# Block-sparse attention and MoE on one core: computing 352 of 768 key columns per query tile, with the division behind the product with the values

## The chip, the cores and the metric

The kernel runs on one core of a Trainium2 chip. A core has five engines with a queue each: TensorE (PE, with PEld for its weight loads), VectorE (DVE), ScalarE (ACT), GpSimd (POOL) and SyncE (SP, which here only issues DMAs). The metric is the device time of one execution in microseconds; smaller is better. The kernel before took 878.65 us in the median of three runs (877.41 to 878.98).

## The reference

Four batches, eight heads, 768 positions, head dimension 64. Attention is masked by blocks of 32 positions: a query block sees its neighbours, the first and the last block, and three sampled blocks; the first and the last query block see everything. The result goes through a two-layer network with a parametric ReLU. Q, K and V are float32, the weights float64, the sampled blocks int64.

```python
scores = scale * np.matmul(q, k.transpose(0, 1, 3, 2))
mask = np.abs(blk_i - blk_j) <= window
mask = mask | (blk_i == 0) | (blk_j == 0) | (blk_i == n_blocks - 1) | (blk_j == n_blocks - 1)
for qb in range(n_blocks):
    for kb in sampled_blocks[qb]:
        mask[qb * block:(qb + 1) * block, kb * block:(kb + 1) * block] = True
scores = np.where(mask, scores, -1000000000.0)
attn = np.exp(scores - np.max(scores, axis=-1, keepdims=True))
attn = attn / (np.sum(attn, axis=-1, keepdims=True) + 1e-09)
x = np.matmul(attn, v)      # then (3072, 512): tokens x heads * 64
h = x @ w_in                # 512 x 2048
out = (np.maximum(h, 0.0) + alpha * np.minimum(h, 0.0)) @ w_out
```

## The kernel before

**Numbers.** float32 is carried as a pair of float16 parts, upper and lower, after a scaling by a power of two. A product is the sum of three (MoE, values) or four (scores) float16 products in the same PSUM. For the scores, upper and lower parts of a head lie side by side on the 128 partitions, and `ks` is K with its two halves swapped: Q against `kt` and against `ks` gives all four terms.

**Attention.** A unit is two heads, with two tiles of 128 queries; a step is one head and one tile, 192 in all. A step multiplies Q with all 768 keys (`emit_s`, L558: four matmuls of 512 and 256 columns), adds the mask and finds the extreme in one VectorE instruction (`emit_bias`, L568), takes the exponential on ScalarE (L575), makes the reciprocal of the sum (L579, L583), makes upper and lower parts of the normalised probabilities (`emit_p_hi`, L348/L350/L352; `emit_p_lo`, L356 on VectorE or L358 and L359 on GpSimd; a table `PL` sends two of three to GpSimd) and transposes both by DMA on SP's queue (L598). `emit_av` (L633) then multiplies with V for a whole unit: 36 matmuls with 64-wide weights, the two heads in the two halves of the array. The output lies transposed already, as the MoE needs it (`x`, L644 and L649).

**MoE.** A chunk is two query tiles with all eight heads (12 chunks). Eight times it does an up block (`emit_up`, L947: 24 matmuls of 256 columns into `h`, of which there is one buffer), `emit_act` on VectorE (L957, L958), the upper part `gh` on ScalarE (L963), the lower part `gl` on GpSimd (L968), and a down block (`emit_down`, L986: 12 matmuls of 512 columns).

**The start.** The weights come as float64, 512 KB a piece, and are made into float32 by integer steps (`emit_n1`, `emit_n2`, `emit_n3`: L805, L812 or L810, L817) on VectorE, then into float16 parts (`emit_w_hi`, `emit_w_lo`; for `w_in` the lower part goes over TensorE, L873 and L874). K and Q of the first units are transposed by TensorE (L480, L483, L498).

**Order.** Nothing of the order is written out by hand. Every piece of work is a `plan.op` with a priority, a cost per engine, its dependences and its buffers; `Plan.run` plays these through with its own costs and so fixes each engine's order. On the chip each engine then takes its instructions strictly in that order. The buffer counts stand in `BUFS` (L42) and in the PSUM pools (L211 to L215).

## Time and profile before

| | |
|---|---|
| runs | 878.65 us in the median of three, 877.41 to 878.98 |
| profiled execution | span 876.4 us from its first to its last instruction; the profile gives no other time of its own |
| mean granted TensorE clock | 0.961 |
| DMA packets | 381844, 133.80 MB |

The profile is one execution on the chip. Its page gives each engine's busy time, the span in 40 slices, the DMA queues, and groups of instructions by line. "Windows" give busy times in chosen stretches, the "timeline" instructions in order, "waits" who waited for whom. In rows of the timeline the first two numbers are start and duration in us; a matmul's duration contains its way through the array, so its price in a stream is the distance from start to start.

### The profile page before, as it was taken

What the parts mean: (1) busy time and instruction counts of PE and PEld (TensorE: products, weight loads), DVE (VectorE), ACT (ScalarE), POOL (GpSimd) and SP (SyncE); (2) the same over time, 40 slices, a digit from 0 to 9 for tenths busy, and PEclk for the clock granted to TensorE, in tenths of its full rate; (3) what the DMA queues carried; (4) which work ended last, traced back from release to release, by engine and by line L of the source; (5) the groups of instructions that cost most, each with busy time, mean ns of one, the idle gap of its engine ahead of it and who ended that gap; (6) DMA issues with size and microseconds to landing.
All of it is one profiled execution on the core that took longest, in us unless ns stands there. A gap on an engine that the chain in (4) does not pass through costs nothing.

```text
span 876.4 us, 17097 instructions
## 1 busy us (share of the span) xinstructions
PE 802.7 (92%) x6249; PEld 533.7 (61%) x6249; DVE 672.0 (77%) x1395; ACT 554.9 (63%) x1188; POOL 560.4 (64%) x458
## 2 busy tenths in 40 slices
PE   3856476999999999999999999999999999999997
PEld 2423134666766666676666666667666666766664
DVE  3889989999977778779877777788787787666322
ACT  4886677877656777566746866666667774565111
POOL 3294676777846786767757867667467867666121
PEclk9878567999999999999999999999999999999999
DMA  7877778799799797877889979888997986776200
GB/s 234 243 189 188 195 156 149 125 171 169 167 174 172 145 176 142 182 144 145 187 154 177 148 149 155 179 143 163 189 183 142 175 132 114 122 132 109 37 25 25
DMA packets 381844, 133.80 MB, mean 153 GB/s; under 512 B 346404, under 2 KB 375104, under 8 KB 381760
## 3 DMA queue, kind: packets, MB, share of 16 engines
q1 hardware_dynamic: 345728, 90.74, 61.1%
q10 hardware_dynamic: 35968, 41.95, 16.7%
q8 instruction: 49, 0.80, 0.4%
q14 instruction: 35, 0.29, 0.1%
q0 software_dynamic: 64, 0.02, 0.0%
HBM read 35.67 MB, written 6.29 MB: 48 GB/s over the span
## 4 chain that ended last, share of the span: by engine, by line
PE 63%; DVE 14%; issue 8%; POOL 6%; ACT 6%; ACTq 2%; DMA 1%; POOLq 0%; DVEq 0%
PE h L947 21%; PE o L986 21%; PE sp L558 10%; PE av L633 8%; DVE e L568 2%; ACT e L575 2%; POOL ph L359 2%; ACTq L387 2%; POOL gl L968 2%; DVE wo L817 1%; DVE g L957 1%; POOL e L358 1%; ACT ph L348 1%; DVE g L958 1%; DVE qn L426 1%
## 5 line engine op out<-in xcount | busy, mean ns | idle before, releaser
L947 PE MATMUL h<-x,wi 128*128 128x256 f16 x2304 | 267.2, 273 | 7.3 <-DVE g L958 7.3
L947 PEld LDWEIGHTS <-wi 128*128 128x128 f16 x2304 | 225.0, 98 | 47.9 <-issue 10.2
L986 PE MATMUL o<-wo,gh 128*128 128x512 f16 x768 | 228.5, 379 | 0.0
L575 ACT ACTIVATE e<-e,nm 128x768 f32<-128x768 f32 x192 | 178.6, 930 | 74.6 <-DVE nm L568 65.7
L359 POOL TENSOR_TENSOR ph<-e,ph 128x768 f16<-128x768 f32 x128 | 217.9, 1702 | 10.7
L568 DVE CUSTOM_DVE_ANT_0 e<-sp,bias,cs 128x768 f32<-128x768 f32 x192 | 192.0, 1007 | 26.2 <-PE sp L558 16.6
L358 POOL TENSOR_SCALAR e<-e,rs 128x768 f32<-128x768 f32 x128 | 132.0, 1032 | 110.4 <-ACT ph L348 60.4
L968 POOL TENSOR_TENSOR gl<-g,gh 128x512 f16<-128x512 f32 x96 | 117.9, 1228 | 115.0 <-ACT gh L963 107.4
L963 ACT CAST gh<-g 128x512 f16<-128x512 f32 x96 | 59.2, 616 | 140.6 <-DVE g L958 130.6
L986 PE MATMUL o<-wo,gl 128*128 128x512 f16 x384 | 145.5, 379 | 0.6 <-POOL gl L968 0.6
L957 DVE TENSOR_SCALAR g<-h,am 128x256 f32<-128x256 f32 x192 | 83.6, 476 | 78.5 <-PE h L947 78.1
L558 PEld LDWEIGHTS <-qt 128*128 128x128 f16 x768 | 74.2, 102 | 84.9 <-issue 32.1
L986 PEld LDWEIGHTS <-gh 128*128 128x128 f16 x768 | 74.7, 98 | 78.6 <-issue 0.8
L558 PE MATMUL sp<-kt,qt 128*128 128x512 f16 (+1 forms) x384 | 98.9, 341 | 21.6 <-DVE nm L568 19.4
L348 ACT ACTIVATE ph<-e,rs 128x768 f16<-128x768 f32 x110 | 101.6, 926 | 12.3 <-DVE rs L583 5.8
L633 PE MATMUL av<-pt,v 128*64 128x256 f16 x1728 | 105.9, 278 | 0.0
L633 PEld LDWEIGHTS <-v 128*64 128x64 f16 x1728 | 92.1, 111 | 18.9 <-issue 16.1
L558 PE MATMUL sp<-ks,qt 128*128 128x512 f16 (+1 forms) x384 | 98.4, 339 | 0.0
L356 DVE SCALAR_TENSOR_TENSOR ph<-e,rs,ph 128x768 f16<-128x768 f32 x64 | 76.6, 1197 | 11.1 <-ACT ph L348 10.6
L958 DVE SCALAR_TENSOR_TENSOR g<-h,gsc,g 128x512 f32<-128x512 f32 x96 | 72.1, 751 | 3.4
L986 PEld LDWEIGHTS <-gl 128*128 128x128 f16 x384 | 37.6, 98 | 46.3 <-POOL gl L968 1.1
L352 POOL TENSOR_SCALAR ph<-e,rs 128x768 f16<-128x768 f32 x38 | 45.1, 1186 | 30.5 <-DVE rs L583 21.7
(132 smaller groups left out, 755.0 us busy)
## 6 DMA issues: line engine op xcount, KB each, us to landing
wo<-in_moe_w_in_dram ACTq DMA_DIRECT2D x16, 512.0 KB, 5.0
raw<-in_moe_w_out_dram ACTq DMA_DIRECT2D x16, 512.0 KB, 4.0
kf<-in_k_dram ACTq DMA_DIRECT2D x16, 384.0 KB, 4.2
qf<-in_q_dram ACTq DMA_DIRECT2D x48, 128.0 KB, 4.3
vf<-in_v_dram ACTq DMA_DIRECT2D x16, 384.0 KB, 5.2
out_dram<-ob ACTq DMA_DIRECT2D x24, 256.0 KB, 4.2
ks<-kt SPq DMA_DIRECT2D x24, 192.0 KB, 3.9
pt<-ph SPq DMA_TRANSPOSE x192, 3.9
```

The source lines that it names most:

```text
L348: nc.scalar.activation(dst, src, AF.Copy, scale=scale)
L358: nc.gpsimd.tensor_scalar(tmp, src, scale, 1.0, ALU.mult, ALU.mult)
L359: nc.gpsimd.tensor_tensor(dst, tmp, hi, ALU.subtract)
L558: nc.tensor.matmul(T["sp", n][:, a:z], T["qt", u][:, h, i, :], kt[:, h, a:z], start=(x == 0), stop=(x == 1))
L568: nc.vector.tensor_tensor_reduce(T["e", n], T["sp", n], bias[:, t0 + j % w, :], scale=T["cs", c][:, hp : hp + 1], scalar=3.0e38, op0=ALU.a ...
L575: nc.scalar.activation(T["e", n], T["e", n], AF.Exp, bias=T["nm", n], scale=-1.0, accum_out=T["su", n])
L633: nc.tensor.matmul(av[h * D : (h + 1) * D, : n * P], v2[:, h, t, vv, :], T["pt", u, h][:, pl * NT + t, :], start=(m == 0), stop=(m == len( ...
L947: nc.tensor.matmul(ph[:, i, :], win(w, f, ct), x[:, ct, :], start=(m == 0), stop=(m == len(terms) - 1))
L957: nc.vector.tensor_scalar(g[:, i, :], ph[:, i, :], 0.0, am1[:, f : f + 1], ALU.min, ALU.mult)
L958: nc.vector.scalar_tensor_tensor(g, ph, gsc[:, j : j + 1], g, ALU.mult, ALU.add)
L968: nc.gpsimd.tensor_tensor(T["gl", c, j], T["g", c, j], T["gh", c, j], ALU.subtract)
L986: nc.tensor.matmul(T["o", c][t], g[:, i, t * P : (t + 1) * P], wout(w, f), start=(f == 0 and m == 0), stop=(f == NF - 1 and m == 2),)
```

## The change

Query tiles are shifted by one block. The tiles t = 0 to 4 of a batch hold the query blocks 4t+1 to 4t+4, so that their neighbours are six consecutive key blocks; tile 5 holds the blocks 21, 22, 23 and 0 and stays dense. A unit is now one tile with four heads (48 units: 40 sparse, 8 dense).

A sparse tile has 352 score columns: 192 of neighbours and 64 of the first and last block, straight from `kt` (`emit_s`), and 3 x 32 sampled ones. The sampled keys differ for each of the four query blocks: `emit_kr` copies them on GpSimd, 12 copies a unit with addresses from registers, and `emit_r` multiplies each with the 32 queries that it belongs to, in a 32-wide part of the array. Sampled columns that the other parts hold already are masked. V's parts are written to DRAM once per batch (`emit_v_out`); from there `emit_vr` gathers the sampled blocks with 12 DMAs a unit on SP's queue, and `emit_vb` reads the other blocks. In the product with the values the probabilities are now the weights and V the moving operand, 128 columns (V's two parts) and 64 a time; PSUM holds queries x heads.

The probabilities are not divided any more, only scaled by a constant. The division comes after the values: a sum of the two halves (`emit_x_sum`), a product with the reciprocal (`emit_x_mul`), both parts (`emit_x_hi`, `emit_x_lo`) and a DMA transpose (`emit_x_t`). The step L579 goes.

Q is swapped instead of K (`qs` by DMA). K, V and Q are read in rows of one head, 256 bytes. K and Q of the start are transposed by DMA like all others. The PSUM buffers for scores become four of one bank, where they were two of two banks. The sums of squares write into a spare part of `wi`.

What moves, at three places of the engines' order. On TensorE, in the middle of the run, before: the last of a step's scores (`sp`, from Q's `qt` with `kt` and `ks`) and the first of a down block.

```order
L558 MATMUL sp<-kt,qt 128x512
L558 LDWEIGHTS qt
L558 MATMUL sp<-kt,qt 128x256
L558 LDWEIGHTS qt
L558 MATMUL sp<-ks,qt 128x512
L558 LDWEIGHTS qt
L558 MATMUL sp<-ks,qt 128x256
L986 LDWEIGHTS gh
L986 MATMUL o<-wo,gh 128x512
```

In the change, at such a place: the last head's scores of a sparse unit and the first of its 32 gathered ones (`kr`).

```order
L555 MATMUL sp<-kt,qt 128x192
L555 LDWEIGHTS qt
L555 MATMUL sp<-kt,qt 128x64
L555 LDWEIGHTS qs
L555 MATMUL sp<-kt,qs 128x192
L555 LDWEIGHTS qs
L555 MATMUL sp<-kt,qs 128x64
L555 LDWEIGHTS qt
L555 MATMUL sp<-kr,qt 32x96
```

A head's two long pairs became two pairs of 192 and 64 columns, and eight matmuls of 96 columns and 32 queries come behind. In all, TensorE's matmuls for scores and values go from 2496 to 4736.

On VectorE, before, the last rows ahead of the first MoE result (`g`): lower halves of `w_out` (`wo`), bias steps (L568) and a lower half of probabilities (`ph`).

```order
L649 SCALAR_TENSOR_TENSOR x<-av,x 128x256
L356 SCALAR_TENSOR_TENSOR wo<-wo,s_wo 128x512
L583 RECIPROCAL rs<-dn 128x1
L568 ISA e,nm<-sp,bias,cs 128x768
L568 ISA nm 128x1
L356 SCALAR_TENSOR_TENSOR wo<-wo,s_wo 128x512
L356 SCALAR_TENSOR_TENSOR ph<-e,rs,ph 128x768
L957 TENSOR_SCALAR g<-h,am_124 128x256 x2
```

And in the change:

```order
L364 SCALAR_TENSOR_TENSOR wo<-wo,s_wo 128x512
L688 TENSOR_REDUCE xf<-av 128x256
L364 SCALAR_TENSOR_TENSOR ph_101<-e,ph_101 128x2x352
L693 TENSOR_TENSOR xf<-xf,rs 128x256
L635 ISA e,nm<-sp,bias,cs 128x352
L635 ISA nm 128x1
L1059 TENSOR_SCALAR g<-h,am_146 128x256 x2
```

Ahead of the first `g` stand all 16 lower halves of `w_out`, where 6 stood before, 28 bias steps of 352 columns for 24 of 768, and the pieces of the division (`xf`).

On GpSimd in the middle of the run, before: lower halves of probabilities (two instructions each) between the lower halves of `g`.

```order
L968 TENSOR_TENSOR gl<-g,gh 128x512
L358 TENSOR_SCALAR e<-e,rs 128x768
L359 TENSOR_TENSOR ph<-e,ph 128x768
L352 TENSOR_SCALAR ph<-e,rs 128x768
L968 TENSOR_TENSOR gl<-g,gh 128x512
```

In the change, at such a place, with the beginning of a gather (a load of registers, then 12 pairs of an address step and a copy):

```order
L693 TENSOR_TENSOR xf<-xf,rs 128x256
L1068 TENSOR_TENSOR gl<-g,gh 128x512 x3
L360 TENSOR_SCALAR v_7508<-vf,sv 128x12x64
L1068 TENSOR_TENSOR gl<-g,gh 128x512
L526 TENSOR_LOAD sidx
L528 ISA
L550 COPY kr<-kt 128x4x32
```

Nearly all lower halves of probabilities went to VectorE (106 of 112, before 64 of 192), and gathers took their place; a `gl` stands right behind 28 of the 40 gathers.

The diff, cut to its core:

```diff
-BUFS = {"wr": 2, "vf": 4, "qf": 4, "qt": 3, "qn": 2, "ph": 4, "e": 4, "pt": 4, "x": 2, "g": 3, ... "kt": 4, "ks": 4, "v2": 4, "gh": 3, "gl": 3}
+BUFS = {"vf": 4, "qf": 1, "qn": 1, "qt": 2, "qs": 2, "ph": 4, "e": 3, "pt": 5, "xf": 1, "xn": 2, "x": 3,
+        "g": 3, "sid": 1, "kt": 3, "v2": 3, "vb": 2, "vr": 2, "kr": 2, "gh": 3, "gl": 3}
...
-    q_nat = [q[b].rearrange("h (p t) d -> p h t d", t=NT) for b in range(B)]
-    k_nat = [k[b].rearrange("h (p t) d -> p h (t d)", t=NT) for b in range(B)]
-    v_nat = [v[b].rearrange("h (p t) d -> p h (t d)", t=NT) for b in range(B)]
+    q_tok = [q[b].rearrange("h s d -> s h d") for b in range(B)]
+    k_nat = [k[b].rearrange("h (t p) d -> p h t d", p=P) for b in range(B)]
+    v_nat = [v[b].rearrange("h (t p) d -> p t h d", p=P) for b in range(B)]
...
+    units = [(b, t, c) for b in range(B) for t in range(NT) for c in range(NQ)]
...
+    def picks(eng, name, t, use):
+        regs = [eng.alloc_register(name=f"{name}{i}") for i in range(NG4 * NR)]
+        eng.load(regs, sidx[0:1, 4 * t + 1 : 4 * t + 1 + NG4].rearrange("p a r -> p (a r)"))
+        for i, reg in enumerate(regs):
+            use(i // NR, i % NR, eng.snap(reg, min_val=0, max_val=NBLK - 1))
...
+        def use(g, r, i):
+            nc.sync.dma_start(
+                vr[r * BLK : (r + 1) * BLK, g], scr[bass.ds(i * BLK, BLK), c * HQ : (c + 1) * HQ, :]
+            )
...
+        def use(g, r, i):
+            nc.gpsimd.tensor_copy(kr[:, :, g, r * BLK : (r + 1) * BLK], kt[:, :, bass.ds(i * BLK, BLK)])
...
+    def mm(dst, lhs, rhs, start):
+        nc.tensor.matmul(dst, lhs, rhs, start=start, stop=False, skip_group_check=True)
+
+    def emit_s(u, h):
+        b, t, c = units[u]
+        T["sp", u, h] = sp = ps_s.tile([P, 512], F32, tag="s", name="sp")
+        kt = T["kt", b, c][:, h]
+        for x, key in enumerate(("qt", "qs")):
+            lhs = T[key, b, t][:, c * HQ + h, :]
+            mm(sp[:, CA:CG], lhs, kt[:, t * P : t * P + CG], x == 0)
+            mm(sp[:, CG:CR].rearrange("p (n j) -> p n j", j=BLK), lhs,
+               kt.rearrange("p (n j) -> p n j", j=BLK)[:, 0 : NBLK : NBLK - 1, :], False)
...
+    def emit_r(us, uv):
+        if us is not None:
+            b, t, c = units[us]
+            for h in range(HQ):
+                for key in ("qt", "qs"):
+                    for g in range(NG4):
+                        r = slice(g * BLK, (g + 1) * BLK)
+                        mm(T["sp", us, h][r, CR:CS], T[key, b, t][:, c * HQ + h, r], T["kr", us][:, h, g, :], False)
+        if uv is not None:
+            new_av(uv)
...
+                        if x == 0:
+                            mm(av[r, h].rearrange("p a d -> p (a d)"), lhs, rhs, h == 0)
+                        else:
+                            mm(av[r, h, 0], lhs, rhs[:, :D], False)
+
+    def av_mm(u, h, pt, x, i, v, start):
+        av = av_view(u)
+        mm(av[:, h].rearrange("p a d -> p (a d)"), pt[:, 6 * x + i, :], v, start)
+        mm(av[:, h, 0], pt[:, 6 * x + 3 + i, :], v[:, :D], False)
...
-            T["e", n], T["sp", n], bias[:, t0 + j % w, :], scale=T["cs", c][:, hp : hp + 1], scalar=3.0e38,
-            op0=ALU.add, op1=ALU.min, accum_out=T["nm", n],
+            T["e", u, h // 2][:, h % 2, :CS], T["sp", u, h][:, :CS], bias[:, t], scale=T["cs", b, t][:, c : c + 1],
+            scalar=3.0e38, op0=ALU.add, op1=ALU.min, accum_out=T["nm", u, h],
...
-    def emit_dn(n):
-        T["dn", n] = new_small("dn")
-        nc.scalar.activation(T["dn", n], T["su", n], AF.Identity, bias=eps, scale=1.0 / PSCALE)
...
-        times(e, T["ph", n][:, 0, :], T["e", n], T["rs", n])
+        times(e, T["ph", u, x][:, :, 0, :w], T["e", u, x][:, :, :w], PSCALE)
...
+    def emit_x_sum(u):
+        T["xf", u] = wt("xf", [P, HQ, D], F32)
+        av = T["av", u].rearrange("p (h a d) -> p h d a", h=HQ, a=2)
+        nc.vector.tensor_reduce(T["xf", u], av, AX.X, ALU.add)
...
+        eng.tensor_tensor(xf, xf, T["rs", u].unsqueeze(2).broadcast_to([P, HQ, D]), ALU.mult)
...
-        o = plan.op(n - 1, lo, lambda e: emit_p_lo(e, n), [o], [], [pb, eb])
+            o = plan.op(4 * u + 2 * x - 1, {"DVE": (0.87, 0), "POOL": (1.0, 1.5)}, lambda e, x=x: emit_p_lo(e, u, x), [o], [], [pb, eb])
...
+        T["okr", u] = plan.op(n - 4, {"POOL": 5.0}, lambda: emit_kr(u), o_kt[b, c] + gate_k, [T["krb", u]], [kbuf[b, c]])
+        T["ovr", u] = plan.op(n - 3, {"SP": 1.5}, lambda: emit_vr(u), o_scr[b] + gate_v, [T["vrb", u]], dma=1.6)
```

More of the change, by code (lines that the diff above doesn't have):

```diff
@@ L69, in __init__ @@
         self.ops, self.free = [], dict(pools)
+        self.slots = {x: list(range(n)) for x, n in pools.items()}
     def buf(self, *pools):
@@ new lines, in mask_dense, with spread @@
+    def mask_dense():
+        for r in range(NR):
+            nc.vector.scalar_tensor_tensor(dtab, bcol, sf[:, TS, r : r + 1], dtab, ALU.is_equal, ALU.max)
+    def spread(dst, src):
+        n = src.shape[-1]
+        nc.scalar.activation(
+            dst.rearrange("p (n j) -> p n j", j=BLK), src.unsqueeze(2).broadcast_to([P, n, BLK]),
+            AF.Copy, bias=NEG, scale=-NEG,
+        )
+    o = plan.op(-20, {"POOL": 6.0}, lambda: None)
+    o_r = plan.op(-18, {"DVE": 1.2}, mask_random, [o])
@@ L335, in pow2 @@
+    o_d = plan.op(0, {"DVE": 0.3}, mask_dense, [o])
+    o_bias = [plan.op(-12 + 5 * t, {"ACT": 0.55}, lambda t=t: spread(bias[:, t], btab[:, t]), [o_r]) for t in range(TS)]
+    o_bias.append(plan.op(8, {"ACT": 0.95}, lambda: spread(dbias, dtab), [o_d]))
     def pow2(ss, u, s):
@@ L756, in values @@
[L756 to L768 removed]
+        o_scr[b] = []
```

977 lines of the change are left out of this document (505 added, 472 removed).

## The prediction

> **What bounds the kernel now.** I read the page first: shares of the span, then the slices (each digit is a tenth of a slice of 21.9 us).
>
> ```profile
> span 876.4 us, 17097 instructions
> PE 802.7 (92%) x6249; PEld 533.7 (61%) x6249; DVE 672.0 (77%) x1395; ACT 554.9 (63%) x1188; POOL 560.4 (64%) x458
> PE   3856476999999999999999999999999999999997
> ```
>
> TensorE is part busy for seven slices, then full to the end. The timeline places the border: the first block of the MoE's up product starts at 152.23. I asked for the busy times on each side of it, and in one stretch inside the start.
>
> ```profile
> 152.23 2.78 PE L947 MATMUL h<-x,wi 128*128 128x256 f16 x24
> ...
> core 0: us, PE busy (x) PEld busy (x) DVE busy (x) ACT busy (x) POOL busy (x), PEclk, DMA share, GB/s
> 75.00:100.00 25.00, 12.25 (x62) 6.02 (x61) 24.90 (x45) 16.79 (x39) 13.67 (x10) 0.78 0.66 174
> ...
> 0.00:152.20 152.20, 91.55 (x511) 48.46 (x512) 128.03 (x275) 107.61 (x240) 86.96 (x84) 0.78 0.77 194
> ...
> 152.20:876.40 724.20, 711.17 (x5740) 485.21 (x5738) 544.02 (x1121) 447.29 (x949) 473.44 (x375) 1.00 0.79 144
> ```
>
> So there are two stages. The start is VectorE's (24.9 of 25 us): it turns the float64 weights into f32 and f16. From 152.2 on TensorE works 711 of 724 us at full clock, and its waits in the whole run are small:
>
> ```profile
> PE sp L558 <- DVE nm L568: 19.4, 13, 5.0
> PE h L947 <- DVE g L958: 7.3, 9, 2.1
> ```
>
> The second stage changes only by TensorE's work, the start by VectorE's or the DMA's. What VectorE, ScalarE and GpSimd save after 152 us is worth nothing by itself.
>
> **The second stage: TensorE's work.** Steady prices stand in the timeline: from start to start a score step (rows 401.98 to 402.63) takes 0.65 us, a values block (405.35 to 407.44) 2.09. Up and down blocks are from the chain.
>
> ```profile
> 401.98 0.49 PE L558 MATMUL sp<-kt,qt 128*128 128x512 f16 x2
> ...
> 402.63 2.78 PE L947 MATMUL h<-x,wi 128*128 128x256 f16 x24
> 405.35 2.16 PE L633 MATMUL av<-pt,v 128*64 128x256 f16 x36
> 407.44 0.50 PE L558 MATMUL sp<-kt,qt 128*128 128x512 f16 x2
> ...
> 160.53 2.59 PE o L986 x12
> ...
> 165.96 2.62 PE h L947 x24
> ```
>
> In the order of before, 167 of 192 score steps and 44 of 48 values blocks stand behind the first up block: 167 x 0.65 + 44 x 2.09 = 200.6 us, beside 96 x (2.62 + 2.59) = 500.2. That makes 700.8 of the 711 busy.
>
> The change leaves the 500.2. Behind its first up block stand 129 sparse score heads, 33 blocks of gathered scores, 35 of gathered values, 35 sparse values blocks and the 32 dense heads (scores and values). A score step streams 1536 columns in 0.65 us, 0.42 ns each. Fewer columns go with many more matmuls: a sparse unit (4 heads of 128 queries) has 96, where 4 steps of before had 52. The cost of a short matmul decides; the nearest rows are K's transposes in the start, at full clock:
>
> ```profile
> 27.69 0.53 PE L483 MATMUL kp<-ident,kn 128*64 128x128 f16 x12
> 28.15 0.50 PE L558 MATMUL sp<-kt,qt 128*128 128x512 f16 x2
> ...
> 27.69 0.36 PEld L483 LDWEIGHTS <-kn 128*64 128x64 f16 x12
> ...
> 30.28 0.65 PEld L480 LDWEIGHTS <-kn 128*128 128x128 f16 x11 [0.60 <-issue]
> ```
>
> Twelve matmuls of 128 columns, 64 wide, take 0.46 us: 38 ns each where 128 columns alone are 54, so neighbouring column tiles overlap. Their weight loads go at 30 ns each; full 128-wide loads at no more than 59.
>
> Gathered blocks: 32 matmuls, 32 wide, of 64 to 128 columns. Four overlapping tiles need 7 to 14 ns of streaming each, so loads or issue set the pace. I take the 30 ns row; bounds are 15 (half, for half as wide a load) and 59. The values block of before, 2.09 against 36 x 53 ns, shows 0.17 for entering and leaving the narrow mode; I add 0.1 a block. So 32 x 0.030 + 0.1 = 1.06 us (0.6 to 2.0), 68 blocks: 72 us (40 to 136). The Trainium skill, "TensorEngine Tiling (Array Packing)", Instruction Overhead, gives every matmul some 60 cycles however short. No run here shows that; at the 0.42 ns of a column it would be 25 ns (an estimate), and the sum 11 us lower.
>
> The other short ones stream 64 columns (27 ns) behind a full load, so 27 to 59 ns; I take 43. Sparse scores: 0.217 for 512 columns plus two exposed loads, 0.245 a head (0.217 to 0.281), 31.6 us. Sparse values: 8 pairs of 128 and 64 columns, 0.78 (0.65 to 0.94), 27.3. Dense scores are as before, 32 x 0.65 = 20.8; dense values 6 pairs a head, 0.59 (0.49 to 0.71), 18.9. Together 170.6 us (128 to 249) against 200.6: **-30 us**, from -73 to +48. The columns alone would promise more; short matmuls take back over half.
>
> What else could make TensorE wait: from a unit's gathered scores to its gathered values the order has 12 to 40 us of other TensorE work, and the transposes between land in 3.9 us (below). VectorE loses 192 x 1.0 us of bias steps but takes over most lower halves from GpSimd (106 of 112), a reduction, a product and a subtraction per unit: I estimate that it stays near its 544 us. Its queue is as full as before, so I add **+4** (0 to 25) of waits.
>
> **The start.** What VectorE does before the first up block's result:
>
> ```profile
> L568 DVE CUSTOM_DVE_ANT_0 e<-sp,bias,cs 128x768 f32<-128x768 f32 x25 | 24.8, 1005 | 0.4 <-PE sp L558 0.4
> L817 DVE SCALAR_TENSOR_TENSOR wo<-raw,wo 128x512 int32<-128x512 int32 x16 | 15.8, 988 | 0.0
> L817 DVE SCALAR_TENSOR_TENSOR wi<-wo,wi 128x512 int32<-128x512 int32 x16 | 13.1, 817 | 0.8 <-ACT wo L810 0.8
> L805 DVE TENSOR_SCALAR wo<-raw 128x512 int32<-128x512 int32 x16 | 9.5, 602 | 0.0
> L356 DVE SCALAR_TENSOR_TENSOR wo<-wo,s_wo 128x512 f16<-128x512 f32 x6 | 6.3, 1054 | 0.6 <-ACT wo L348 0.6
> L649 DVE SCALAR_TENSOR_TENSOR x<-av,x 128x256 f16<-128x256 f32 x4 | 1.7, 422 | 1.1 <-ACT x L644 1.1
> ...
> L805 DVE TENSOR_SCALAR wo<-raw x16: 411/415/1861, 68.7 to 130.1; 128x512 int32<-128x512 int32 x16
> L817 DVE SCALAR_TENSOR_TENSOR wo<-raw,wo x16: 667/680/2118, 71.4 to 134.7; 128x512 int32<-128x512 int32 x16
> L356 DVE SCALAR_TENSOR_TENSOR wo<-wo,s_wo x16: 740/762/2129, 141.3 to 189.7; 128x512 f16<-128x512 f32 x16
> L359 POOL TENSOR_TENSOR ph<-e,ph x128: 1638/1646/2226, 35.9 to 809.3; 128x768 f16<-128x768 f32 x128
> ```
>
> Means lie far above medians (min/median/max): 602 over 415, 988 over 680, with maxima near GpSimd's two-input step of 1646. Some weight steps sat that step out; GpSimd has 19 two-input steps in the start now and 2 in the changed order. At medians the 64 steps of L805 and L817 cost 13 us less. Bias steps: 28 of 0.61 (422 for 256 columns, 1005 for 768, so 0.53 for 352, and 0.08 for the read of the minimum) against 25 of 1.09: -10. In front now stand all 16 lower halves of wo, not 6 (+6 at medians), and by the same rows some +15 in all for six more lower halves of probabilities, four more weight steps, wo's upper halves, V, masks and the division's pieces, less the copies of K. Net -2; without the relief up to +23.
>
> The DMA is the other side. K and V of batch 0 come in 12288 pieces of 256 bytes, not 2048 of 1536; K and Q are transposed by DMA, and V goes out to DRAM and back.
>
> ```profile
> q1 hardware_dynamic: 345728, 90.74, 61.1%
> q10 hardware_dynamic: 35968, 41.95, 16.7%
> ...
> pt<-ph SPq DMA_TRANSPOSE x192, 3.9
> ```
>
> That is 61.1% x 876.4 x 16 / 345728 = 24.8 ns a packet on the transposing queue and 65 on the loading one. At 24.8 the loads cost 19 us of 16 engines against 8 (50 at 65); 88 transposed tiles of 132 packets (345728 / 2624 tiles of 128 x 128) 18, V's round trip some 16 (3968 pieces of 1 or 2 KB at 65 ns), nine fewer transposes of probabilities (12 tiles each) -22. The share of 0.77, 117 of 152 us, becomes about 140: covered, without much room. I take **+3** for the start, from -8 to +30. Over the whole run the transposes fall by 704 of 2624 tiles (-143 us), and the gathered V, its copies, and the small pieces of K, V and Q give about as much back: the DMA's load stays.
>
> **Sum.** 876.4 - 30.5 + 3 + 4 = 852.9 us of span. The median of the three runs, 878.65, is 2.25 above the span (what lies around it): 855.
>
> **Rivals.** *Short matmuls do not overlap.* The 68 gathered blocks run at 59 ns a matmul (2.0 us each, +63), and full loads bound the rest (+14): 932, slower. It decides from 41 ns on: the 23.5 us gained, over 2176 matmuls, is 11 ns each. For it: a new weight load before every matmul, and four tiles at once that no row shows. Against: the 38 ns row. 0.11.
>
> *Every full load takes as long as an up matmul,* 109 ns (2.62 / 24, one load each): scores 56, sparse values 61, dense values 42 instead of 32, 27 and 19: +81, 936. The 59 ns row speaks plainly against it: 0.02. The Trainium skill's "TensorE: Matmul & The Clock Gate", section LDWEIGHTS, has it as columns / 1.2, 107 ns; by that rule the trace differs, and the row decides.
>
> *The start grows:* loads at 65 ns a piece and V's round trip fill the DMA, and the first up block comes 30 us late: 882. It decides from +27. 0.15.
>
> *GpSimd's gather holds the lower halves of g.* A down block needs gl, which now queues behind 12 copies.
>
> ```profile
> L297 POOL CAST ident<-ident 128x128 f16<-128x128 f32 x1 | 0.3, 280 | 0.0
> L868 POOL TENSOR_SCALAR sid<-ident,ssc 128x128 f32<-128x128 f32 x8 | 6.1, 759 | 7.6 <-DVE ssc L339 4.1 <-PE d L873 3.5
> L968 POOL TENSOR_TENSOR gl<-g,gh 128x512 f16<-128x512 f32 x96 | 117.9, 1228 | 115.0 <-ACT gh L963 107.4 <-PE o L986 7.6
> L957 DVE TENSOR_SCALAR g<-h,am 128x256 f32<-128x256 f32 x192 | 83.6, 476 | 78.5 <-PE h L947 78.1
> L958 DVE SCALAR_TENSOR_TENSOR g<-h,gsc,g 128x512 f32<-128x512 f32 x96 | 72.1, 751 | 3.4
> L963 ACT CAST gh<-g 128x512 f16<-128x512 f32 x96 | 59.2, 616 | 140.6 <-DVE g L958 130.6 <-DVE rs L583 9.9
> ```
>
> Of equal size, the cast takes 0.28, sid 0.76: 3.4 to 9.1 us a gather, plus its address steps, which no row shows. A down block, an up block (5.2 us) and some attention (170.6 / 96 = 1.8) cover g's way to gl. With a gather of 9 us just begun when gh is ready, gl comes 9.1 + 1.2 us after the 2.3 of L957 (two), L958 and L963: 5.6 us late, and 1 us late with the gather half done. 28 gathers have a gl right behind: 30 to 157 us, as they fall; I price it at 45, 900. Below some 6 us a gather is hardly seen. 0.09.
>
> *Better:* 18 ns a short matmul takes another 26 us off: 829. 0.13.
>
> **Chances.** The forecast case has 0.50, its own range 835 to 876. About 0.2% (1.8 us) is what a measurement of this kernel can tell from no change. Faster: 0.48 + 0.13 + 0.03 of the late start = 0.64; same: 0.02 of each of those = 0.04; slower: 0.10 + 0.11 + 0.02 + 0.09 = 0.32. The range, 815 to 905, leaves out the matmul rivals and an extreme of the better case.
>
> **What would show it.** In the changed profile: a gathered block of 32 matmuls near 1.06 us; the first up block near 155 us; TensorE 9 in every slice behind it, some 682 us of work there; L805's successors at medians near 415 with few long ones; gathers of 4 to 6 us. Wrong would be: a block over 1.4 us, a first up block past 179, or waits of TensorE behind gl or gathered K of more than 20 us.

## The result and the profile after

The changed kernel takes 1017.5 us (median of 4 runs, 1012.7 to 1018.9); the kernel before, measured beside it, 878.6. The ratio is 1.158 (95% interval 1.155 to 1.161): **slower by 139 us**, where the prediction had 855 us.

The page of the changed kernel, the rows that answer to those of before:

```profile
span 1015.6 us, 22541 instructions
PE 761.2 (75%) x7931; PEld 510.4 (50%) x7931; DVE 638.9 (63%) x1535; ACT 374.7 (37%) x854; POOL 330.0 (32%) x676
PE   1455422777896888596897886895987787979998
PEclk9976555889898799798897987897998998989999
```

Every engine that the page counts does less than before, and none is full: TensorE has fallen from 92% to 75%, VectorE from 77% to 63%. Work that shrinks on every engine while the time grows means waiting. The slices show it: behind the eighth, before had nines but for the last, now they run from 5 to 9, and the granted clock moves with them. The first up block now starts at 183.5 us; the busy times on both sides of it (TensorE, its weight loads, VectorE, ScalarE, GpSimd, then TensorE's clock):

```profile
0.00:183.00 183.00, 68.24 (x676) 42.34 (x677) 127.89 (x314) 84.40 (x198) 62.82 (x167) 0.70 0.81 196
183.00:1015.60 832.60, 693.00 (x7259) 468.01 (x7256) 511.05 (x1221) 290.31 (x656) 267.18 (x509) 0.90 0.65 125
```

That divides the 139.2 us by which the span grew (1015.6 - 876.4):

| part | before | after | difference |
|---|---|---|---|
| start, to the first up block | 152.0 | 183.0 | +31.0 |
| second stage, TensorE waits | 13.0 | 139.6 | +126.6 |
| second stage, up and down blocks | 531.7 (clock 1.00) | 572.4 (clock 0.90) | +40.6 |
| second stage, other TensorE work | 179.7 | 120.6 | -59.0 |

(The waits are length less busy time; up and down blocks are the busy times of their two lines in that stretch, and the last row is the rest.) So attention became cheaper on TensorE by twice what was forecast, and waits ate that and more. What TensorE waits for behind 183 us, the five longest (us in total, times, longest); before, the largest behind 152 us was 7.3 us in total, for `g`:

```profile
PE av L555 <- DMA pt<-ph: 51.0, 19, 8.9
PE o L1085 <- POOL gl L1068: 25.4, 11, 6.2
PE sp L555 <- DMA qs<-qt: 16.3, 3, 7.3
PE sp L555 <- DVE nm L649: 15.2, 10, 3.2
PE h L1050 <- DVE g L1060: 14.8, 8, 5.5
```

The first and the third were not in the list before. Both are transfers that SyncE issues: the transposes of the probabilities, and the swapped queries. The DMA engines are not the reason (0.65 busy in that stage, 0.79 before), and a transpose of probabilities does not take much longer once it is issued (4.2 us from issue to landing, 3.9 before). So I looked at SyncE's own queue, which counts as busy in no table (timeline of SyncE; then the load of registers by its line, min/median/max in ns):

```profile
566.15 3.27 SPq L683 DMA_TRANSPOSE pt<-ph  x2
569.52 1.62 SPq L708 DMA_TRANSPOSE x<-xn  x1
574.21 7.09 SPq L538 DMA_DIRECT2D vr<-scr  x12
581.41 1.47 SPq L683 DMA_TRANSPOSE pt<-ph  x1
582.92 1.63 SPq L426 DMA_TRANSPOSE qt<-qn  x1
584.65 1.22 SPq L708 DMA_TRANSPOSE x<-xn  x1
585.98 1.29 SPq L683 DMA_TRANSPOSE pt<-ph  x1
```

```profile
L526 SPq TENSOR_LOAD <-sidx x40: 2469/3074/4513, 80.5 to 896.5; - x40
```

There is no gap in this stretch: SyncE goes from one instruction to the next. Between the end of the output's transpose (571.14) and the end of the twelve transfers (581.30) stand 10.2 us, 3.07 of them without a row here: the load of the twelve registers (L526). Then four transposes come one behind the other; the last of what they read was written at 569.66, 12 to 16 us before they are issued. This gather of values costs 10.2 us of SyncE, 40 such ones 406 us; the planner had written its order for 1.5 us each. Behind the first up block the gaps of over 0.25 us between SyncE's instructions come to 99 us of 832, 44 of them one wait for the output at the end; before it was 260 of 724, 39 of them at the end. (A row can itself contain a wait, so SyncE may be somewhat less full than this says.)

### The profile page after: what moved, and what is told of

It is laid out like the page before. It is cut to its first block, busy times and chain, and to the rows that moved or that the text cites. A ratio compares the mean times of both kernels' runs of the same rounds, so it can differ in the third digit from the quotient of the medians.

```text
span 1015.6 us, 22541 instructions
## 1 busy us (share of the span) xinstructions
PE 761.2 (75%) x7931; PEld 510.4 (50%) x7931; DVE 638.9 (63%) x1535; ACT 374.7 (37%) x854; POOL 330.0 (32%) x676
## 4 chain that ended last, share of the span: by engine, by line
PE 32%; issue 13%; DMA 9%; DVE 8%; SPq 5%; POOL 3%; ACT 2%; POOLq 1%; ACTq 1%; DVEq 0%
PE h L1050 13%; PE o L1085 12%; PE sp L555 4%; DMA pt<-ph 3%; PE av L555 3%; SPq L538 2%; POOL gl L1068 2%; SPq L526 2%; DVE g L1059 2%; DVE ph L364 1%; POOL kr L550 1%; DMA qs<-qt 1%; DVE g L1060 1%; DMA x<-xn 1%; DMA qt<-qn 1%
## 5 line engine op out<-in xcount | busy, mean ns | idle before, releaser
L550 POOL COPY kr<-kt 128x128 f16 x480 | 153.4, 374 | 179.2 <-PE sp L555 128.2
L1059 DVE TENSOR_SCALAR g<-h,am 128x256 f32<-128x256 f32 x192 | 83.8, 478 | 139.2 <-PE h L1050 132.8
L642 ACT ACTIVATE e<-e,nm 128x352 f32<-128x352 f32 x160 | 92.6, 579 | 79.3 <-DVE nm L635 47.0
L364 DVE SCALAR_TENSOR_TENSOR ph<-e,ph 128x704 f16<-128x704 f32 (+1 forms) x106 | 102.7, 976 | 25.2 <-ACT ph L356 25.0
L555 PEld LDWEIGHTS <-pt 96*32 96x32 f16 (+1 forms) x2304 | 74.0, 106 | 77.3 <-DMA pt<-ph 58.6
L555 PE MATMUL sp<-kt,qt 128*128 128x192 f16 (+2 forms) x384 | 67.1, 257 | 55.7 <-DVE nm L635 40.1
L635 DVE CUSTOM_DVE_ANT_0 e<-sp,bias,cs 128x352 f32<-128x352 f32 x160 | 86.8, 575 | 20.8 <-PE sp L555 20.7
L555 PE MATMUL sp<-kt,qs 128*128 128x192 f16 (+2 forms) x384 | 67.7, 259 | 16.3 <-DMA qs<-qt 16.3
L555 PEld LDWEIGHTS <-qt 128*32 128x32 f16 (+1 forms) x1024 | 46.7, 104 | 62.7 <-issue 34.8
L555 PEld LDWEIGHTS <-qs 128*32 128x32 f16 (+1 forms) x1024 | 45.3, 104 | 38.8 <-issue 19.7
L356 ACT ACTIVATE ph<-e 128x704 f16<-128x704 f32 (+1 forms) x62 | 49.7, 804 | 32.6 <-DMA pt<-ph 17.9
## 6 DMA issues: line engine op xcount, KB each, us to landing
vf<-in_v_dram ACTq DMA_DIRECT2D x48, 128.0 KB, 5.0
qs<-qt SPq DMA_DIRECT2D x48, 128.0 KB, 2.7
```

The costliest lines, as they stand in the source:

```text
L356: nc.scalar.activation(dst, src, AF.Copy, scale=scale)
L364: nc.vector.scalar_tensor_tensor(dst, src, scale, hi, ALU.mult, ALU.subtract)
L550: nc.gpsimd.tensor_copy(kr[:, :, g, r * BLK : (r + 1) * BLK], kt[:, :, bass.ds(i * BLK, BLK)])
L555: nc.tensor.matmul(dst, lhs, rhs, start=start, stop=False, skip_group_check=True)
L635: nc.vector.tensor_tensor_reduce(T["e", u, h // 2][:, h % 2, :CS], T["sp", u, h][:, :CS], bias[:, t], scale=T["cs", b, t][:, c : c + 1], s ...
L642: nc.scalar.activation(e, e, AF.Exp, bias=T["nm", u, h], scale=-1.0, accum_out=su_of(u)[:, h : h + 1])
```

## The experiments

**Theory S:** SyncE's queue. The gather of values keeps it for 10 us at a time, transposes behind it are late, TensorE waits, and its clock falls with the waits. **Rivals:** *G*, GpSimd's gather of keys holds gl and the scores; *O*, the planner's order is wrong, because its costs for both gathers are far from the real ones.

All kernels, each timed beside the kernel before on the same chip (877.1 to 879.5 us). The kernels with `static`, `fixed` or `load_4` in their names, and scores_first, read fixed blocks in place of the sampled ones: they leave out the choice, and show only what its time is worth.

| kernel | us | ratio to before (95%) | first up block at |
|---|---|---|---|
| changed | 1017.5 | 1.158 (1.155-1.161) | 183.5 |
| v_static | 892.3 | 1.012 (1.006-1.018) | 175.2 |
| k_static | 1004.1 | 1.141 (1.138-1.144) | 182.5 |
| kv_static | 885.4 | 1.007 (1.005-1.009) | 167.9 |
| true_costs | 1037.3 | 1.179 (1.177-1.182) | 161.6 |
| v_12_fixed | 921.1 | 1.047 (1.044-1.050) | 173.1 |
| v_load_4 | 890.6 | 1.017 (1.012-1.023) | 173.3 |
| v_load_once | 969.2 | 1.105 (1.101-1.108) | 177.7 |
| before_sp | 1012.1 | 1.150 (1.147-1.154) | 162.3 |
| v_ind | 991.2 | 1.132 (1.126-1.137) | 189.2 |
| v_ind_same | 964.1 | 1.097 (1.090-1.104) | 183.0 |
| ind_once_alpha | 955.2 | 1.089 (1.084-1.094) | 185.6 |
| split | 959.3 | 1.092 (1.090-1.094) | 180.5 |
| pair | 938.4 | 1.066 (1.062-1.070) | 186.4 |
| alpha_first | 1017.9 | 1.160 (1.156-1.163) | 185.1 |
| sid_dve | 1011.4 | 1.150 (1.146-1.154) | 180.0 |
| v_load_4_sid | 888.7 | 1.009 (1.006-1.012) | 168.8 |
| scores_first | 893.3 | 1.014 (1.011-1.017) | 177.6 |
| v_static_div | 924.0 | 1.054 (1.051-1.057) | 175.9 |

### Which gather, or the order?

v_static and k_static replace one gather each by fixed reads, kv_static both:

```diff
...
-            nc.sync.dma_start(
-                vr[r * BLK : (r + 1) * BLK, g], scr[bass.ds(i * BLK, BLK), c * HQ : (c + 1) * HQ, :]
-            )
-        picks(nc.sync, f"v{u}_", t, use)
+        for g in range(NG4):
+            nc.sync.dma_start(vr[:, g], scr[:KR, c * HQ : (c + 1) * HQ, :])
...
-            nc.gpsimd.tensor_copy(kr[:, :, g, r * BLK : (r + 1) * BLK], kt[:, :, bass.ds(i * BLK, BLK)])
-        picks(nc.gpsimd, f"k{u}_", t, use)
+        for h in range(HQ):
+            nc.gpsimd.tensor_copy(kr[:, h], kt[:, h, : NG4 * KR].rearrange("p (g k) -> p g k", g=NG4))
```

> Leaves out the gather of values: SyncE reads the first 96 rows of the scratch four times a block with fixed addresses (4 transfers, no load of registers) in the place of a load of 12 registers and 12 addressed transfers; everything else, the order on every engine too, is that of the changed kernel. Theory S (the gather holds SyncE's queue for some 10 us a block and the transposes of the weights, the queries and the outputs behind it come late): some 8 us of SyncE are gone in each of 40 blocks, TensorE's waits for pt, qs and x shrink to under 30 us in all, 900 to 950 us. Theory G (GpSimd's gather holds gl and the scores): within 15 us of the changed kernel, 1003 to 1018. Theory O (the order written by the planner is wrong for the real times wherever it is): about half of the loss stays, 950 to 1000.

> Leaves out the gather of keys: GpSimd copies the first 384 columns of each head's keys in 4 fixed copies a block, without a load of registers; the order on every engine is that of the changed kernel. Theory S: 1000 to 1018 us, since SyncE's queue is as full as before. Theory G: the wait of TensorE for gl (25 us) goes, and with it the blocks that wait for kr: 930 to 980 us. Theory O: 990 to 1018.

> Leaves out both gathers, with the edits of the two kernels before it together. Theory S: as with the values' gather alone, 900 to 950 us. Theory G: as with the keys' alone. If the sum of both matters, under 900 us, and what is left above the time that the forecast gave (855) is the start and the lower granted clock.

Measured: 892.3, 1004.1 and 885.4. Without the values' gather the time falls by 125 us, and 139 had been lost; without the keys' it falls by 13, or by 7 where the values' is gone already. S holds, though 892 and 885 lie under its range of 900 to 950; G is real and small.

true_costs changes two numbers of the planner:

```diff
# in two plan.op lines
-... {"POOL": 5.0} ...
+... {"POOL": 7.5} ...
-... {"SP": 1.5} ...
+... {"SP": 10.5} ...
```

> Computes all that the changed kernel computes; only the two costs by which the planner orders the work are those of the trace: 7.5 in the place of 5.0 for the gather of keys on GpSimd, and 10.5 in the place of 1.5 for the gather of values on SyncE. Theory O: the order now fits the chip, 900 to 960 us. Theory S: SyncE's work is the same, only ordered around; 970 to 1015 us. Theory G: 980 to 1015.

Measured: 1037.3, 20 us slower than the changed kernel and above the range of all three theories. The order with honest costs brought the first up block forward to 161.6, and lost more behind it. O falls as the main cause as far as this planner goes: told the real costs, it finds no better order. That there is none was not shown.

### What in the gather: the registers or the transfers?

v_12_fixed keeps twelve transfers at fixed addresses and drops the load; v_load_4 was meant to keep the load and issue four; v_load_once loads the registers once for both groups of heads:

```diff
 # v_12_fixed
+                i = (5 * u + 7 * g + 3 * r) % NBLK
+                nc.sync.dma_start(vr[r * BLK : (r + 1) * BLK, g], scr[i * BLK : (i + 1) * BLK, c * HQ : (c + 1) * HQ, :])
 # v_load_4
+        picks(nc.sync, f"v{u}_", t, lambda g, r, i: None)
+        for g in range(NG4):
+            nc.sync.dma_start(vr[:, g], scr[:KR, c * HQ : (c + 1) * HQ, :])
 # v_load_once
+        if c == 0:
+            nc.sync.load(T["vreg", b, t], sidx[0:1, 4 * t + 1 : 4 * t + 1 + NG4].rearrange("p a r -> p (a r)"))
```

> Leaves out the choice of the value blocks: the load of 12 registers is gone and the 12 transfers a block stay, 32 rows each, at addresses fixed in the program. Theory L (the load of registers, 3.07 us a block on SyncE, is what delays the rest): 3.1 of the 7.7 us a block that the kernel with 4 fixed transfers saved are saved here; if the gain goes with SyncE's time, 50 of its 125 us, so 965; if the load alone is to blame, 895. Theory N (the number of transfers, 0.575 us of SyncE each): 940 to 1000.

> Leaves out the choice of the value blocks too: the load of 12 registers a block stays, its values are not used, and 4 fixed transfers of 96 rows take the place of the 12. Theory N: 8 x 0.575 = 4.6 us a block are saved; if the gain goes with SyncE's time, 75 of the 125 us, so 943; if the transfers alone are to blame, 895. Theory L: 980 or more. If this and the kernel with 12 fixed transfers gain together more than 125 us, the first microseconds taken from SyncE are worth more than the last, and the queue was past its limit.

> Computes all that the changed kernel computes: SyncE loads the 12 registers once for a tile of queries and uses them for both groups of heads, so that 20 loads of 3.07 us are left of 40 (61 us of SyncE less). If SyncE's time is what counts, at the rate of the fixed kernel (125 us gained for 307 us of SyncE) some 25 us are gained, 992; below 960 if the queue was only just past its limit. Within 5 us of 1017 if the loads fall where SyncE would wait anyway.

Measured: 921.1, 890.6 and 969.2. v_load_4 is not the test that it was meant to be: nothing uses its registers, and its trace has no load on SyncE. In the load's place stand 40 semaphore instructions of 17 ns, and between the end of the transpose ahead of a gather and its first transfer there are 0.17 us:

```profile
L526 SPq EVENT_SEMAPHORE  x40: 17/17/17, 80.7 to 762.2; - x40
```

```profile
408.69 1.27 SPq L426 DMA_TRANSPOSE qt<-qn  x1
410.13 1.86 SPq L539 DMA_DIRECT2D vr<-scr  x4
```

So v_load_4 does on SyncE what v_static does, and its time is the same (890.6 and 892.3): it repeats that run, and no run has four transfers with the load. A block's transfers in v_12_fixed:

```profile
418.60 6.03 SPq L540 DMA_DIRECT2D vr<-scr  x12
```

| kernel | SyncE for the gather, one block | 40 such blocks | gained |
|---|---|---|---|
| changed | 3.07 + 7.1 | 406 | 0 |
| v_load_once | half of the blocks without 3.07 | 345 | 48 |
| v_12_fixed | 6.0 | 241 | 96 |
| v_load_4 | 1.9 (no load) | 76 | 127 |
| v_static | 1.9 | 76 | 125 |

The first 61 us taken from SyncE give back 48, the next 104 another 48, the last 165 some 30. The first microseconds are worth the most: the more slack the queue has, the more of its work is hidden. Neither L nor N holds alone, but the load weighs more than its share. Over all blocks an addressed transfer starts 0.52 us (median) after the one before it and a fixed one 0.46, so most of what v_12_fixed saves is the load. v_load_once is the cleanest run of the three: it computes all that the changed kernel does, with the same transfers and the same order on every other engine, and 20 loads less give 48 us. So it is SyncE's time that counts, and not the DMA traffic.

In v_load_4 the second stage shows what the change does with that queue relieved (windows of the start and of the second stage, then TensorE's two largest waits behind it):

```profile
0.00:173.00 173.00, 66.52 (x678) 41.71 (x679) 127.79 (x314) 84.39 (x198) 60.99 (x167) 0.73 0.92 210
173.00:883.60 710.60, 654.38 (x7256) 451.03 (x7254) 510.67 (x1222) 290.04 (x656) 269.88 (x509) 0.98 0.77 146
```

```profile
PE sp L552 <- DVE nm L646: 15.2, 11, 3.7
PE o L1082 <- POOL gl L1065: 12.8, 10, 3.1
```

pt and qs are gone from the list, the waits are 56 us instead of 140, the clock is 0.98, and the stage is 14 us shorter than before's 724.4. (This execution is 5 us below its kernel's median; v_static's, 2.5 us above its own, has 59 us of waits in 717.5.)

### The other side: the same work put into the kernel before

before_sp adds SyncE's work to the kernel before, ahead of one transpose in 40 of its 48 units; for room it has one scratch buffer less for ScalarE's squares:

```diff
+        if j == 0 and u % 6 != 5:
+            nc.sync.load(regs, spick[0:1])
+            for r, reg in enumerate(regs):
+                at = nc.sync.snap(reg, min_val=0, max_val=NBLK - 1)
+                nc.sync.dma_start(junk2[:, r], rows[bass.ds(at * BLK, BLK), :16])
         nc.sync.dma_start_transpose(
```

> The kernel before, with nothing of the change: ahead of one transpose of probabilities in 40 of its 48 units SyncE loads 12 registers and issues 12 transfers with addresses from them (32 rows of 64 bytes into a tile that nobody reads). Its order on every engine is that of the kernel before. Theory S: SyncE has 192 transposes of probabilities of some 1.6 us and some 100 us else, about 410 us; 40 x 10.4 = 416 us more fill 826 of 878, and bunched as they are, transposes come late: 930 to 1000 us. If the changed kernel's loss belongs to its own chain and not to the queue, 880 to 900.

Measured: 1012.1 us, 134 us slower, as good as the whole loss of the change, with none of the change in it. That is above the 930 to 1000 expected, though a block costs SyncE only some 8 us here (twelve transfers take 6.00 us; this load of registers has a median of 1.74). Its waits show the path from the queue to the engines:

```profile
404.01 6.00 SPq L607 DMA_DIRECT2D junk<-in_v_dram  x12
```

```profile
ACT ph L350 <- DMA pt<-ph: 72.7, 23, 8.4
POOL ph L354 <- DMA pt<-ph: 57.8, 9, 9.9
```

The next split of probabilities needs the buffer (ph) that a late transpose still reads. In the kernel before, ScalarE had no such row, and GpSimd's came to 0.4 us behind 152 us. S is shown from both sides.

### A complete kernel with a free SyncE

v_ind lets GpSimd fetch the rows by indirect transfers, with a table of row numbers worked out once and one scratch tensor for each group of heads; v_ind_same is the same with the planner's old cost and old rule for free buffers, so the order of TensorE, VectorE and ScalarE is that of the changed kernel:

```diff
-        picks(nc.sync, f"v{u}_", t, use)
+        for g in range(NG4):
+            nc.gpsimd.indirect_dma_start(
+                vr[:, g].rearrange("p h a -> p (h a)"), None, T["scr", b, c].rearrange("s h a -> s (h a)"),
+                bass.IndirectOffsetOnAxis(vidx[:, 4 * t + 1 + g : 4 * t + 2 + g], 0),
+            )
```

> Computes all that the changed kernel computes: the values are gathered by 4 indirect transfers a block that GpSimd issues (96 rows each, row numbers from a table worked out once), in the place of SyncE's load and 12 transfers; the scratch is one tensor for each group of heads, and the planner counts 5 us of GpSimd for it. Theory S: SyncE is as free as with 4 fixed transfers, so 880 to 930, unless GpSimd takes over 10 us a block for its four, which would bring GpSimd to some 330 + 400 of 900 us and hold gl: then 950 to 1000. Theory O (the order is wrong): 960 or more.

> Computes all that the changed kernel computes, by the indirect transfers on GpSimd of the kernel v_ind (0.924 us each, 4 a block), but the planner counts them as it counted SyncE's gather, so that every engine's other instructions stand in the changed kernel's order. Theory S (a free SyncE is what matters, and the order is good once the queue is): 885 to 930. Theory G2 (GpSimd's own 4.9 us a block, 195 us in all, hold gl and the copies of keys): 960 to 1000, like v_ind. If it is faster than v_ind by 40 us or more, the order that the planner wrote with 5 us of GpSimd, and not GpSimd's time, made v_ind slow.

Measured: 991.2 and 964.1. The order alone is worth 27 us: v_ind lies where O had put it (960 or more), and an honest cost gave the worse order here as in true_costs. v_ind_same lies in G2's 960 to 1000 and over S's 885 to 930. The waits for pt and qs are gone from TensorE's list; in their place GpSimd holds the lower halves of g:

```profile
L548 POOL DMA_INDIRECT vr<-scr,vidx x160: 916/922/1525, 82.7 to 850.9; - x160
```

```profile
PE o L1094 <- POOL gl L1077: 50.1, 22, 8.4
```

Rival G's mechanism, with 50 us of waits instead of 25: the load was moved from one in-order queue into another. ind_once_alpha loads the keys' registers once for a tile of queries (and alpha first), split shares the values' gather between SyncE and GpSimd, pair lets SyncE gather all eight heads at once:

```diff
 # ind_once_alpha, split, pair
+        if c == 0:
+            nc.gpsimd.load(T["kreg", b, t], sidx[0:1, 4 * t + 1 : 4 * t + 1 + NG4].rearrange("p a r -> p (a r)"))
 # pair
-                vr[r * BLK : (r + 1) * BLK, g], scr[bass.ds(i * BLK, BLK), c * HQ : (c + 1) * HQ, :]
+                vr[r * BLK : (r + 1) * BLK, g], scr[bass.ds(i * BLK, BLK), :, :]
```

> Computes all that the changed kernel computes: the kernel v_ind_same, with alpha loaded first and with GpSimd's 12 registers for the keys loaded once for a tile of queries (20 loads of 2.7 us in the place of 40). If GpSimd's time holds gl in v_ind_same, 54 us of GpSimd less give 10 to 30 us beside the start's 5 to 10: 860 to 910. If not, 5 to 10 us below v_ind_same.

> Computes all that the changed kernel computes: the values of the first group of heads are gathered by SyncE (20 loads of registers and 240 transfers), those of the second by GpSimd's indirect transfers (80 of 0.924 us), the registers for the keys are loaded once for a tile of queries, the diagonals of scales are made on VectorE. SyncE is relieved by 20 x 10 = 200 us, more than the 8 fixed kernels needed; GpSimd has 98 us more and 54 us less. Theory S with P: 885 to 920. If GpSimd's part holds gl as in v_ind_same (50 us of waits with 195 us more), 920 to 945.

> Computes all that the changed kernel computes: SyncE gathers the values of all eight heads at once, 20 loads of 12 registers and 240 transfers of 64 KB in the place of 40 and 480, so some 208 us of SyncE less; the registers for the keys are loaded once for a tile of queries, the diagonals of scales made on VectorE; for the room, one buffer less each for transposed probabilities (4), x (2) and gl (2), so the planner writes another order. Theory S: as with 4 fixed transfers, 885 to 905, if the order is as good; the orders that the planner wrote for other costs were worse by 20 to 30 us (true_costs, v_ind), then 905 to 940. Over 950 would say that SyncE's time is not what counts.

Measured: 955.2, 959.3 and 938.4, none at the low end. ind_once_alpha is 9 us under v_ind_same, as its second case had it, with 43 us of waits for gl left. split lies over both of its ranges; TensorE waits little for any one thing in it (19.5 us for gl at most behind its start), but for many. pair is the best complete kernel, 79 us under the changed one, in the range for a worse order; it needed one buffer less in three places and got another order, and how much each of these keeps it from 890 was not tried. No kernel here beats the kernel before, not even those with fixed blocks.

### The start

In the start VectorE does the same work as before, 127.9 us (128.0), spread over 31 us more. Two waits in the trace looked like causes: VectorE's second instruction waits 11.6 us for alpha, and TensorE for the diagonal of scales that GpSimd makes behind two gathers (GpSimd, then TensorE):

```profile
43.15 3.43 POOL L550 COPY kr<-kt 128x128 f16 x12 [2.60 <-issue]
49.68 6.84 POOL L550 COPY kr<-kt 128x128 f16 x12 [3.11 <-issue]
...
60.11 0.37 POOL L972 TENSOR_SCALAR sid<-ident,ssc 128x128 f32<-128x128 f32 x1
```

```profile
60.53 2.08 PE L977 MATMUL d<-wi,sid 128*128 128x512 f32 x2 [8.59 <-POOL sid L972]
```

```diff
 # alpha_first: this line moved ahead of the loads of sampled blocks
     nc.gpsimd.dma_start(al_r, alpha.rearrange("(f p) -> f p", p=P))
 # sid_dve, v_load_4_sid
-        T["sid", g] = wt("sid", [P, P], F32)
+        T["sid", g] = work.tile([P, P], F32, tag="sid", name="sid", bufs=2)
-        nc.gpsimd.tensor_scalar(T["sid", g], ident, ssc[:, g : g + 1], 1.0, ALU.mult, ALU.mult)
+        nc.vector.tensor_scalar(T["sid", g], ident, ssc[:, g : g + 1], None, ALU.mult)
 # scores_first, on top of v_load_4_sid (wlo: the lower halves of weights on TensorE)
+    for o in wlo[4:8]:
+        o.deps += T["oss", 0] + T["oss", 1]
```

> Computes all that the changed kernel computes; GpSimd issues the load of alpha ahead of its nine loads of sampled blocks instead of behind them. VectorE's second instruction waits 11.6 us for it through TensorE's transposition. If the start is VectorE's work in order, 5 to 10 us come off the first up block (183.4 us) and off the time: 1007 to 1012. If the start waits for loads, values or other engines by then, within 3 us of 1017.

> Computes all that the changed kernel computes; the eight diagonals of scales for the weights are made on VectorE (about 0.2 us each, two buffers) at the place in the order where GpSimd made them behind its gathers of keys. Theory P (this wait, 8.6 us and what follows it, delays the first scores from some 50 to 68 us): the first up block comes at 160 to 175 us in the place of 183.4, and the time falls by 8 to 20 us, 997 to 1010. If the start is held by something else (the registers' load of the values, the 128 us of VectorE work), within 4 us of 1017.

> Leaves out the choice of the value blocks as v_load_4 does (4 fixed transfers a block), with the diagonals of scales on VectorE as in sid_dve. If the two queues are the two causes of the loss, the forecast's terms come out: first up near 160 us, 870 to 880 us. If the start stays at 173, 888 to 895.

> Leaves out the choice of the value blocks, as v_load_4_sid does, its twin; the planner may place the lower halves of weights five to eight on TensorE only behind the scores of the first two units, so those are computed some 10 us earlier. If the late first scores carry the start: the first scores near 53 us in the place of 65, the first up block near 160 in the place of 169, 875 to 882 us. If VectorE's work in the order in which it stands carries it: the first up block between 165 and 175, 883 to 895.

Measured: 1017.9 with the first up block at 185.1, no gain. The wait for alpha did shrink, but the next instruction then waits for a table of GpSimd (`bq`). VectorE's second and third instructions, changed kernel first:

```profile
12.61 0.17 DVE L994 TENSOR_SCALAR al<-pa 128x16 f32<-128x16 f32 x1 [11.61 <-PE pa L886]
13.77 0.17 DVE L316 TENSOR_TENSOR dd<-sf,bq 128x15 f32<-128x15 f32 x1 [0.98 <-POOL bq L299]
```

```profile
5.88 0.17 DVE L994 TENSOR_SCALAR al<-pa 128x16 f32<-128x16 f32 x1 [4.89 <-PE pa L886]
14.80 0.17 DVE L316 TENSOR_TENSOR dd<-sf,bq 128x15 f32<-128x15 f32 x1 [8.74 <-POOL bq L299]
```

VectorE's work begins no earlier, so what an earlier begin would be worth was not tested. sid_dve moves the first up block by 3.5 us, to 180.0, short of the 160 to 175 expected, and the time by 6; v_load_4_sid has it at 168.8 with 888.7 us, 2 us from its twin's time (v_load_4). scores_first has its first scores at 59.7 us, 5 us before v_load_4_sid (64.8) and not 10, and its first up block comes at 177.6, later than there: earlier first scores don't bring the start forward. So of the 31 us, some 8 to 10 go with the values' gather (183.5 to 175.2 in v_static, 173.3 in v_load_4), 4.5 with the diagonals (173.3 to 168.8), and 17 stay open. The DMA may hold them: its share in v_load_4's start is 0.92 (before: 0.77). No run took the transfers of the start away, so that is not shown.

### The division behind the product

v_static_div puts the division back ahead of the split, in v_static, where SyncE is free:

```diff
+            nc.vector.tensor_scalar(rs, su, 1e-9, 1.0 / PSCALE, ALU.add, ALU.mult)
+            nc.vector.reciprocal(rs, rs)
...
+            times(e, T["ph", u, x][:, d, 0, :w], src, rs)
...
-        eng.tensor_tensor(xf, xf, T["rs", u].unsqueeze(2).broadcast_to([P, HQ, D]), ALU.mult)
+        eng.tensor_scalar(xf, xf, 1.0 / PSCALE, 1.0, ALU.mult, ALU.mult)
```

> Leaves out the gather of values as v_static does, and undoes the other part of the change: the weights are divided by their sum before they are split (two reciprocals and one scaled split for each head), the product with the values is only scaled by a constant; the order on TensorE is the same. Theory: the wait for the sum comes back into the chain from scores to transposes, 0.3 us for each pair of heads, and VectorE and ScalarE get some 160 instructions more; where v_static's chain has slack, 892 to 900 us; if that chain sets its second stage, 905 to 930.

Measured: 924.0, 32 us over v_static. The second stage, v_static first:

```profile
175.00:892.50 717.50, 658.44 (x7255) 452.93 (x7252) 510.64 (x1222) 289.55 (x656) 269.59 (x509) 0.97 0.76 144
```

```profile
175.00:914.80 739.80, 666.30 (x7264) 456.42 (x7262) 545.16 (x1574) 301.72 (x691) 261.62 (x517) 0.96 0.73 140
```

VectorE gets 352 instructions and 35 us more; TensorE's waits go from 59 to 73 us. The profiled executions show 22 of the 32 us (this one is 7 us under its kernel's median, v_static's 2.5 us over its own). With SyncE free, this half of the change was worth having; part of its price here is that the scaled split takes one instruction for each head, where v_static has one for two.

## Why the prediction was wrong, step by step

**The two stages and what bounds them: right for before, wrong as the ground for after.** "The second stage changes only by TensorE's work" needs slack in every queue. It failed with SyncE's queue near full, and even with SyncE relieved it held only in part: in v_load_4 the waits are 43 us more than before.

**The failed step: the waits of the second stage, +4 us (0 to 25).** The span came out 162.7 us over the 852.9 of the sum, and 122.6 of them are here. The step weighed VectorE's queue, and for the transposes took "3.9 us" from before, the time from issue to landing. It had no term for the time until they are issued. The gather's 40 loads of registers and 480 addressed transfers were counted as DMA traffic, not as SyncE's time in order: 406 us in front of pt, qs, qt and x. Measured: +126.6 us of waits; with SyncE relieved (v_load_4) +43; and SyncE's work alone in the kernel before costs 134 us in all. Those 43 are over the step's range too: TensorE waits there for VectorE's bias steps and activations (19 us for nm, 11 for g; in the second stage of before 8 for both) and for gl (13). The Trainium skill has a figure that speaks for a term here: "Runtime: NRT & Kernel Launch", Instruction fetch mechanics, puts such a load, from HBM, at about 200 ns a register, an estimate of 2.4 us for twelve. The trace, where they come from SBUF, has 2.47 at the least and 3.07 as the median; before_sp, with 0.94 to 2.20, lies under it.

**The same waits cost a second time, through the clock,** which the sum took as 1.00. An up block behind a wait of 5.5 us:

```profile
214.02 5.15 PE L1050 MATMUL h<-x,wi 128*128 128x256 f16 x24 [5.52 <-DVE g L1060]
```

It takes 5.15 us, a steady one 2.78. Over the stage the clock was 0.90, and up and down blocks took 40.6 us more; at 0.98 (v_load_4) they took 12.7 us more. The Trainium skill, "TensorE: Matmul & The Clock Gate", Part 1, says that TensorE falls to half rate after an idle window of about 3.4 us and needs as long a busy one to come back; this row is in line with it: 5.15 us is 2.78 with some 4.7 us at half rate (an estimate from these two rows).

**TensorE's work, -30.5 us (-73 to +48): right in sign, too small.** (Its own lines, 170.6 less 200.6, give -30.0; the matmuls for scores and values are 4352 in the changed kernel, not the 4736 of the section on the change. Neither matters to the result.) The other work of the second stage fell from 179.7 to 110.0 us in v_load_4 (654.4 less 544.4 for up and down blocks): -70, near the bound. The short matmuls are cheaper than the 30 ns row. In v_load_4, a gathered block of scores, and one of values:

```profile
564.39 0.23 PE L552 MATMUL sp<-kr,qt 128*32 128x96 f16 x4
...
564.84 0.61 PE L1082 MATMUL o<-wo,gh 128*128 128x512 f16 x2
...
567.54 0.53 PE L552 MATMUL av<-vr,pt 96*32 96x128 f16 x32
568.00 2.79 PE L1047 MATMUL h<-x,wi 128*128 128x256 f16 x24
```

From start to start 0.45 and 0.46 us for 32 matmuls and 32 loads, 14 ns each: less than half of 1.06, under the bound of 0.6 and under the 25 ns that the prediction also weighed. At 0.46 the 68 blocks cost 31 us in the place of 72, which is about the whole difference. The other short matmuls came near the estimates: a block of sparse values takes 0.68 us behind this up block (0.78 forecast). The rival *Better* (18 ns) was right about this; *Short matmuls do not overlap* and *Every full load* were wrong.

**The start, +3 us (-8 to +30): wrong.** Its first half held: VectorE's work there is 127.9 us (forecast: -2 on 128), and the relief from GpSimd came:

```profile
L909 DVE TENSOR_SCALAR wo<-raw x16: 412/420/479, 91.8 to 136.9; 128x512 int32<-128x512 int32 x16
```

The median is 420 ns as forecast, and the longest 479, not 1861. But work was not what set the start: waits between queues spread it. *The start grows* named the size (30 us) but not the cause: that its DMA fills was not shown, and the values' gather, for which it had nothing, carries about a third. That the size agrees is luck as far as that third goes.

**GpSimd's gather holds gl (0.09):** it does, for 25 us of waits, over the 20 that the text had set as its sign; without the gather the time falls by 13. It is a part beside the cause; with the values' gather moved onto GpSimd (v_ind_same) it became the larger one. Here too the load of registers had no term: 2.7 us in the median, ahead of 3.6 us of copies.

## What to carry to other kernels

Price every instruction in each in-order queue that it is put into, DMA issues and register loads too, and add up that queue's time against the stage, and how long it is held at a time: SyncE's had no row of busy time, and it was the queue that held up the rest. A gather with addresses known only at run time costs its issuer a load and a transfer for every block, whatever it saves in columns. Here fewer loads and fewer, larger transfers gained most (v_load_once 48 us, pair 79); the two orders that the planner wrote for more honest costs were 20 and 27 us worse. When every engine is less busy and the time still grows, look for what the late transfers stood behind.

## What the runs showed of the hardware

- SyncE's load of twelve registers from SBUF takes 3.07 us (median), GpSimd's 2.72; in before_sp SyncE's takes 1.74. From start to start an addressed transfer of 32 rows takes SyncE 0.52 us (median, changed kernel), one at a fixed address 0.46 (v_12_fixed).
- An indirect transfer of 96 rows on GpSimd holds it for 0.92 us, with gaps of 0.30 between; four take 4.7 us (v_ind_same), half of SyncE's twelve with their load (10.2).
- Matmuls 32 wide, four column tiles at a time, follow each other at 14 ns with their own weight loads (v_load_4).
- In before_sp the 480 transfers move 1 MB in all, nobody reads them, and with their 40 loads they cost 134 us: the price is the queue's time, not the bytes.
